# A new order for batch 0 of a Sinkhorn attention and ResMLP kernel: GpSimd products behind the weight loads, K copies and exponentials first, V1 mix inside the first channel layer

## The chip, the cores and the metric

The kernel runs on one core of one Trainium2 chip. The metric is device microseconds (us) of one execution. A profiled execution also shows a span, from the first to the last instruction, which is about 1.8 us shorter than its time. Every execution of the result and of the experiments, and each profile, comes with the mean clock that the TensorE was granted over its span, where 1.0 is full speed.

A run is slow where it is over 1.5% above the fastest of the same kernel in the same call.

## The reference

There are two parts: a sorted block attention and an MLP block that takes its output. Batch is 4, heads 8, sequence 768 in 8 blocks of 96, head size 64, and the MLP width 512.

```python
# attention
P = sort_net                                # 8 x 8 per batch and head
for _ in range(5):                          # exp, then rows and columns normalized
    ...
k_sorted = einsum('bhij,bhjcd->bhicd', P, k_blocks)
v_sorted = einsum('bhij,bhjcd->bhicd', P, v_blocks)
attn = softmax(q_blocks @ k_sorted^T / 8)   # per block of 96
x = attn @ v_sorted                         # -> (batch, 768, 512)
# MLP
a1  = alpha1 * x + beta1
tok = einsum('ts,bsd->btd', w_tok, a1)      # w_tok is 768 x 768
u   = x + lam * tok
a2  = alpha2 * u + beta2
out = u + lam * (relu(a2 @ w_ch1) @ w_ch2)
```

## The kernel before

The tensor engine (PE) works nearly all the time. Batches 1 to 3 run their attention among the channel layers of the batch before, so the PE always has large matmuls at hand. Batch 0 has no batch before it. Its attention consists of small matmuls that wait for one another, and the weight preparation is done in the same stretch: the token weights are copied into a sorted order (`wtp`), turned by the PE (`wtok_ps`) and copied back (`w_tokT`).

In the code, in which some short lines are joined, `pe`, `dve`, `act` and `pool` are TensorE, VectorE, ScalarE and GpSimd. Their instructions stay in program order where `fixed` is set. So the order of the calls below is the order in each engine's queue.

```python
    def prep_affine():                       # two products on GpSimd, 128x512 f32 each
        pool.tensor_tensor(a1lB[:], a1lB[:], lamB[:], ALU.mult)
        pool.tensor_tensor(b1lB[:], b1lB[:], lamB[:], ALU.mult)

    def spin(ps, n):                         # n dummy matmuls, 128x512
        ...

    def load_weights():                      # GpSimd issues these DMAs
        for g in range(4):
            pool.dma_start(W1p[...], ...)
        load_raw(1, 1)
        for g in range(4):
            pool.dma_start(W2p[...], ...)
            if g == 0:
                prep_affine()                # behind the first W2p issue

    def mix_heads(kv, h4, out):              # K or V of batch 0, mixed; two copies out of PSUM
        for lo, hi, copy in ((0, 4, dve.tensor_copy), (4, 6, act.copy)):
            ...

    def sort_wtok(n):                        # two copies SBUF -> SBUF: 128x1152 and 128x384, f16
        for lo, hi, base in ((0, 96, 0), (96, 128, TAIL)):
            dve.tensor_copy(t_[:, :, :, lo:hi], wt16[...])

    def prep_wtok(which, eng):               # six transposes by the PE, one copy PSUM -> SBUF
        for ks in which:
            ...
            eng(w_tokT[:, ks, :], pst[:])

    # ---- order of batch 0 (start cut)
    load_weights()
    mixing_matrices(1)
    turn_v0(0, dve.tensor_copy); mix_k0(0); mix_k0(1); turn_v0(1, dve.tensor_copy)
    sc0(0, 0, 2)                             # scores; the last argument is a number of dummy matmuls
    sc0(0, 1, 2); mix_k0(2); turn_v0(2, dve.tensor_copy)
    sc0(1, 0, 1); pv0(0, 0)                  # pv0: probabilities times V, writes x_ps, then x
    sc0(1, 1, 1); pv0(0, 1); mix_k0(3); turn_v0(3, dve.tensor_copy)
    sc0(2, 0, 1); pv0(1, 0)
    sort_wtok(0)
    sc0(2, 1, 1); pv0(1, 1)
    sort_wtok(1)
    prep_wtok(range(1), dve.tensor_copy)     # the PE waits here for sort_wtok(0)
    sc0(3, 0); pv0(2, 0)
    # ... the rest of w_tokT and x, then the token matmuls tok_ps (128x512)
    mix_v(1, 1, range(0, 4), ...)            # V of batch 1, four of six parts, before the channel layer
    moe_h(0, 0, range(6))                    # first channel layer: h_ps
    mix_v(1, 1, range(4, 6), ...)
    moe_h(0, 0, range(6, HT))
    for kk in range(3):                      # three output blocks (ch_ps) of the first half of batch 0,
        moe_ch(0, 0, (kk,))                  # all before the attention of batch 1
        mix_k(1, gs=(kk,))
        ...
```

The softmax here doesn't subtract the row's maximum and nothing guards it: scores larger than these inputs give would overflow.

Of the kernel before, what the change touches and what calls it, by code (L numbers as in the profile page):

```python
# [16 lines left out]
def kernel(  # L17
# [23 lines left out]
    NB = sort_net.shape[-1]  # L41
# [5 lines left out]
    HT = HID // 128  # L47
# [40 lines left out]
    def psb(shape, dtype, name):  # L88
        return psB.tile(shape, dtype, name=name, tag="psB")
# [63 lines left out]
    def prep_affine():  # L153
        pool.tensor_tensor(a1lB[:], a1lB[:], lamB[:], ALU.mult)
        pool.tensor_tensor(b1lB[:], b1lB[:], lamB[:], ALU.mult)
# [99 lines left out]
    def load_weights():  # L255
        for g in range(4):
            pool.dma_start(W1p[:, :, g * 512:(g + 1) * 512], w1v[:, :, g * 512:(g + 1) * 512])
        load_raw(1, 1)
        for g in range(4):
            pool.dma_start(W2p[:, g * 4:(g + 1) * 4, :], w2v[:, g * 4:(g + 1) * 4, :])  # L260
            if g == 0:
                prep_affine()



# [3 lines left out]
    def mixing_matrices(b):  # L269
        rep = psa([128, NB * NB], FT, "rep_ps")  # L270
        pe.matmul(
            rep[:],
            ebh[:, b, :, :, :].rearrange("p a h j -> p (a h j)"),
            P16[:].rearrange("p i j -> p (i j)"),
            start=True, stop=True,
        )
        sel = att.tile([128, NB, NB], FT, name="sel", tag="sel", bufs=2)
        dve.tensor_tensor(
            sel[:], rep[:].rearrange("p (i j) -> p i j", j=NB),
            mskj[:].unsqueeze(1).to_broadcast([128, NB, NB]), ALU.mult,  # L280
        )
        red = att.tile([128, NB], FT, name="red", tag="red", bufs=2)
        dve.tensor_reduce(red[:], sel[:], AXX, ALU.add)
        big = const([128, 16, NB], F16, f"bigP_{b}")
        dve.tensor_tensor(
            big[:],
            mskb[:].rearrange("p a b -> p (a b)").unsqueeze(2).to_broadcast([128, 16, NB]),
            red[:].unsqueeze(1).to_broadcast([128, 16, NB]),
            ALU.mult,
        )  # L290
        bigP[b] = big
        bgv = const([128, 16, NB], F16, f"bigV_{b}")
        dve.tensor_tensor(
            bgv[:],
            mskv[:].unsqueeze(2).to_broadcast([128, 16, NB]),
            red[:].unsqueeze(1).to_broadcast([128, 16, NB]),
            ALU.mult,
        )
        bigV[b] = bgv
# [74 lines left out]
                    else:  # L374
                        act.copy(dst, src)

    def mix_heads(kv, h4, out):

        raw = raw_of[(0, kv)]
        dst = out.rearrange("p i (t r) -> p t i r", r=16)  # L380
        for lo, hi, copy in ((0, 4, dve.tensor_copy), (4, 6, act.copy)):
            mps = psb([128, hi - lo, 128], FT, "m_ps")
            for t6 in range(lo, hi):
                for h2 in range(2):
                    h = 2 * h4 + h2
                    pe.matmul(
                        mps[h2 * 64:(h2 + 1) * 64, t6 - lo, :], raw[:, h, t6, :],
                        bigH[:, h, :, :].rearrange("p i r -> p (i r)"), start=True, stop=True,
                    )
            copy(dst[:, lo:hi], mps[:].rearrange("p t (i r) -> p t i r", r=16))  # L390

    def mix_k0(h4):
        if 0 not in kT_of:
            kT_of[0] = att.tile([128, H4 * NB, BLK], F16, name="kT", tag="kT", bufs=2)
        mix_heads(0, h4, kT_of[0][:, h4 * NB:(h4 + 1) * NB, :])

    vT0 = []

    def mix_v0(h4):
        vT0.append(moep.tile([128, NB, BLK], F16, name=f"vT_{h4}", tag="u32", bufs=9))  # L400
        mix_heads(1, h4, vT0[h4][:])

    def turn_v0(h4, copy):
        vps = psb([BLK, NB, 2, D], F16, "vt_ps")
        for i in range(NB):
            pe.transpose(vps[:, i, :, :].rearrange("p a d -> p (a d)"), vT0[h4][:, i, :], ident16[:])
        copy(
            Vs[0][:, 2 * h4 * NB:(2 * h4 + 2) * NB, 0:D].rearrange("p (a i) d -> p i a d", a=2), vps[:],
        )
# [46 lines left out]
                    recip[:, lo:hi].unsqueeze(3).to_broadcast([BLK, hi - lo, 2, D]), ALU.mult,  # L456
                )

    def pv_tiles(h4, g, et):

        bank = psb([128, 4, 128], FT, "x_ps")[:].rearrange("p a x -> p (a x)")
        xps = bank[:, 0:6 * GRP].rearrange("p (a i g) -> p a i g", i=3, a=2)
        for rows, cols, i in ((slice(0, BLK), BLK, 0), (slice(BLK, 128), 32, 3)):
            for h2 in range(2):
                for ii in range(3):
                    vi = 3 * g + ii if i == 0 else 6 + g
                    lhsT = et[:, h2, ii, :] if i == 0 else et[:, h2, 3, 32 * ii:32 * ii + 32]
                    pe.matmul(
                        xps[rows, h2, ii, 0:D + 1], lhsT, Vs[0][:, (2 * h4 + h2) * NB + vi, 0:D + 1],
                        start=True, stop=True,  # L470
                    )
        recip = att.tile([128, 2, 3], FT, name="recip", tag="recip0", bufs=3)
        dve.reciprocal(recip[:], xps[:, :, :, D])
        dve.tensor_tensor(
            x_of[0][:, 3 * g:3 * g + 3, h4 * 128:(h4 + 1) * 128].rearrange("p i (a d) -> p a i d", d=D),
            xps[:, :, :, 0:D], recip[:].unsqueeze(3).to_broadcast([128, 2, 3, D]), ALU.mult,
        )
# [26 lines left out]
    def sort_wtok(n):  # L504

        t_ = moep.tile([128, NT, 2, 128], F16, name=f"wtp_{n}", tag="a2T", bufs=3)
        wtp.append(t_)
        for lo, hi, base in ((0, 96, 0), (96, 128, TAIL)):
            w = hi - lo
            dve.tensor_copy(  # L510
                t_[:, :, :, lo:hi],
                wt16[:, :, base + 2 * n * w:base + (2 * n + 2) * w].rearrange("p t (k c) -> p t k c", c=w),
            )
# [10 lines left out]
    def prep_ab2():  # L524
        tps = psb([128, 2 * CT], FT, "ab2_ps")
        pe.transpose(tps[:], ab2[:], ident32[0:2 * CT, 0:2 * CT])
        act.copy(ab2col[:], tps[:])
# [140 lines left out]
    def sc0(h4, g, spins=0):  # L668
        ets[(h4, g)] = emit_scores(0, h4, g, spins)

    def pv0(h4, g):
        pv_tiles(h4, g, ets[(h4, g)])

    x_of[0] = moep.tile([128, NT, C], F16, name="x128", tag="x128", bufs=2)
    mixing_heads()
# [3 lines left out]
    for h4 in range(1, H4):  # L679
        mix_v0(h4)  # L680
    load_weights()
    mixing_matrices(1)
    turn_v0(0, dve.tensor_copy)
    mix_k0(0)
    mix_k0(1)
    turn_v0(1, dve.tensor_copy)
    sc0(0, 0, 2)
    sc0(0, 1, 2)
    mix_k0(2)
    turn_v0(2, dve.tensor_copy)  # L690
    sc0(1, 0, 1)
    pv0(0, 0)
    sc0(1, 1, 1)
    pv0(0, 1)
    mix_k0(3)
    turn_v0(3, dve.tensor_copy)
    sc0(2, 0, 1)
    pv0(1, 0)
    sort_wtok(0)
    sc0(2, 1, 1)  # L700
    pv0(1, 1)
    sort_wtok(1)
    prep_wtok(range(1), dve.tensor_copy)
    sc0(3, 0)
    pv0(2, 0)
    prep_wtok(range(1, 2), dve.tensor_copy)
    sort_wtok(2)
    sc0(3, 1)
    pv0(2, 1)
    prep_wtok(range(2, 4), act.copy)  # L710
    pv0(3, 0)
    prep_wtok(range(4, 5), dve.tensor_copy)
    prep_wtok(range(5, 6), act.copy)
    pv0(3, 1)
    prep_ab2()
    prep_rs()
    moe_start(0)
    moe_row(range(2, NT))
# [4 lines left out]
    for kt in range(2):  # L723
        dve.scalar_tensor_tensor(
            u_of[0][kt][:], b1lB[:], rs[:, kt:kt + 1], x_of[0][:, kt, :], op0=ALU.mult, op1=ALU.add
        )
    moe_tok(0, range(3))
    tok_part(0, 3)
    tok_part(0, 4)
    moe_turn(0, 0)  # L730
    tok_part(0, 5)
    mix_v(1, 1, range(0, 4), (dve.tensor_copy, act.copy))
    pe.fixed = act.fixed = False
    order = [pe.last, act.last]
    moe_tok(0, range(3, NT), done=True)
# [2 lines left out]
    stack = ExitStack()  # L738
    for eng in order:
        stack.enter_context(tc.issue_after(eng.ins))  # L740
    moe_h(0, 0, range(6))
    mix_v(1, 1, range(4, 6), (dve.tensor_copy,))
    pool.tensor_copy(gate[:], Vs[1][0:1, 0, 0:2])
    load_raw(2, 1)
    load_raw(2, 0)
    pool.fixed = False
    moe_h(0, 0, range(6, HT))
    moe_turn(0, 1)
    stack.close()
    pe.fixed = True  # L750
    for kk in range(3):
        moe_ch(0, 0, (kk,))
        mix_k(1, gs=(kk,))
        for h4 in ((0,), (1, 2), (3,))[kk]:
            turn_q(1, h4, dve.tensor_copy)
    pe.fixed = False
    for b in range(1, B):
        if b > 1:
            if b > 2:
                cross_q(b)  # L760
            mixing_matrices(b)
            mix_v(b)
            if b == 2:
                opened = pool.tensor_copy(gate[:], Vs[0][0:1, 0, 0:2])
                with tc.issue_after(opened.ins):
                    load_q(3)
                    load_raw(3, 1)
                    load_raw(3, 0)
            mix_k(b)
        emit_attention(b)  # L770
        if b > 1:
            moe_h(b - 1, 0)
            moe_ch(b - 1, 0)
        moe_h(b - 1, 1)
        moe_a(b)
        moe_ch(b - 1, 1)
        if b == 1:
            load_q(2)
            cross_q(2)
# [33 lines left out]
```

## Time and profile before

| | kernel before |
|---|---|
| time, three runs | 278.16, 278.46, 278.55 us; median 278.46 |
| the profiled run | 282.29 us (span 280.5 us, mean clock 0.975) |
| PE busy | 266.7 us, 95% of the span |
| longest PE wait | 3.67 us, for VectorE's copy wtp, at 27.7 us |
| clock at half speed | from 31.0 to about 44.6 us |
| token matmuls of batch 0 start | 41.90 us |
| token matmuls of batch 1 end | 105.70 us |
| from there to the end | 174.8 us |

These are the head of the page of the kernel before, the PE's line of busy times, and two lines of slices. In the slices each digit stands for a fortieth of the span (7 us); PE is its busy tenths, PEclk its granted clock in tenths.

```profile
span 280.5 us, 5152 instructions
PE 266.7 (95%) x2057; PEld 149.2 (53%) x2057; DVE 160.1 (57%) x332; ACT 126.1 (45%) x233; POOL 92.1 (33%) x100
PE   8889599999999799999999999999999999999993
PEclk9999758999999999999999999999999999999999
```

The PE is 95% busy, so only a little can be gained by filling its gaps. The clock line shows the other loss: in the fifth to seventh slices (28 to 49 us) the PE is granted only 7, 5 and 8 tenths of its speed, and in the sixth and seventh it is called busy all the same.

The timeline of the kernel before around 27 us has the columns start, duration, engine, line, operation, written and read tile, shape, count, and in brackets the idle time before it and what ended it. All operations are recorded in one helper, so the line is always L65 and the tiles tell them apart.

```profile
26.98 0.74 PE L65 MATMUL x_ps<-Vs_96,et 96*96 96x65 f16 x12
...
27.16 4.17 DVE L65 COPY wtp_580<-wt_100 128x1152 f16<-128x1152 f16 x2
...
28.00 1.33 POOL L65 TENSOR_TENSOR a1lB<-a1lB,lamB 128x512 f32<-128x512 f32 x1
29.23 1.31 POOL L65 TENSOR_TENSOR b1lB<-b1lB,lamB 128x512 f32<-128x512 f32 x1
...
31.39 0.82 PE L65 MATMUL wtok_ps<-ident_72,wtp_580 128*128 128x128 f16 x6 [3.67 <-DVE wtp_580 L65]
...
35.02 0.62 DVE L65 COPY wtp_657<-wt_100 128x1152 f16<-128x1152 f16 x2
```

VectorE's two sort copies take 4.17 us. GpSimd's two products (28.00 to 30.54 us) run in that time. The PE has nothing from 27.72 to 31.39 us: it waits for the first sorted tile. The view of that tile gives the shortest, the median and the longest of the two copies, in ns:

```profile
L65 DVE COPY wtp_580<-wt_100 x2: 535/2123/3711, 27.2 to 30.8; 128x1152 f16<-128x1152 f16 x1, 128x384 f16<-128x384 f16 x1
```

The large copy (128x1152) took 3711 ns. The third pair of the same shapes, at 35.02 us where GpSimd does nothing, took 0.62 us for both; there neither copy took more than 0.45 us, against 3.71. This trace shows only that the long copy and the products overlap, not that the products stretch the copy (the collision, below).

The next view is the busy time of the engines in windows of 1 us: window, length, then busy us and number of instructions for PE, PEld, DVE, ACT and POOL, then the granted clock, the DMA share and GB/s.

```profile
30.00:31.00 1.00, 0.00 (x0) 0.00 (x0) 1.00 (x2) 0.00 (x0) 1.00 (x2) 0.97 1.24 207
31.00:32.00 1.00, 0.61 (x6) 0.56 (x6) 0.96 (x4) 0.00 (x0) 1.00 (x3) 0.50 1.23 206
...
44.00:45.00 1.00, 1.00 (x5) 0.35 (x3) 0.48 (x1) 0.75 (x2) 1.00 (x2) 0.70 1.23 205
45.00:46.00 1.00, 1.00 (x7) 0.45 (x5) 0.28 (x2) 0.00 (x0) 1.00 (x2) 1.00 1.27 219
```

The clock falls to 0.50 shortly before the end of the pause (30.9 us, in windows of 0.2 us) and is back at 44.6 us. The matmuls from 31.4 to 41.9 us take longer there: twelve x_ps matmuls 1.06 us instead of 0.67 in the chain.

The waits of the PE (us in total, times, longest) show two more that the change addresses: batch 1's token matmuls wait for x, and the V mix for a copy of itself.

```profile
PE wtok_ps L65 <- DVE wtp_580 L65: 3.7, 1, 3.7
PE tok_ps L65 <- DVE x_1203 L65: 1.4, 2, 0.8
...
PE v_ps L65 <- DVE vA L65: 0.3, 1, 0.3
```

The chain of waits (start, us, what) gives the marks: the start of batch 0's token matmuls and the end of batch 1's.

```profile
41.90 7.88 PE tok_ps L65 x30
...
98.20 7.50 PE tok_ps L65 x34
105.70 10.36 PE ch_ps L65 x48
```

### The profile page before, as it was taken

What the parts mean: (1) busy time and instruction counts of PE and PEld (TensorE: products, weight loads), DVE (VectorE), ACT (ScalarE), POOL (GpSimd) and SP (SyncE); (2) the same over time, 40 slices, a digit from 0 to 9 for tenths busy, and PEclk for the clock granted to TensorE, in tenths of its full rate; (3) what the DMA queues carried; (4) which work ended last, traced back from release to release, by engine and by line L of the source; (5) the groups of instructions that cost most, each with busy time, mean ns of one, the idle gap of its engine ahead of it and who ended that gap; (6) DMA issues with size and microseconds to landing.
All of it is one profiled execution on the core that took longest, in us unless ns stands there. A gap on an engine that the chain in (4) does not pass through costs nothing.

```text
span 280.5 us, 5152 instructions
## 1 busy us (share of the span) xinstructions
PE 266.7 (95%) x2057; PEld 149.2 (53%) x2057; DVE 160.1 (57%) x332; ACT 126.1 (45%) x233; POOL 92.1 (33%) x100
## 2 busy tenths in 40 slices
PE   8889599999999799999999999999999999999993
PEld 2467484555556444455466544554566445545542
DVE  6878947633765898770368386651465874023023
ACT  2456145783358522388056430783076313703700
POOL 8525608800745171502943603400425400000000
PEclk9999758999999999999999999999999999999999
DMA  6999999979999905469999143399210242012012
GB/s 77 184 209 251 212 205 197 182 157 88 154 215 122 106 19 89 115 142 89 137 211 177 37 78 75 90 141 72 76 40 2 47 102 75 2 37 75 2 37 75
DMA packets 62423, 30.88 MB, mean 110 GB/s; under 512 B 48888, under 2 KB 58112, under 8 KB 62400
## 3 DMA queue, kind: packets, MB, share of 16 engines
q0 software_dynamic: 23024, 15.60, 38.6%
q1 hardware_dynamic: 39376, 14.96, 32.5%
q8 instruction: 16, 0.26, 0.4%
q14 instruction: 7, 0.06, 0.1%
HBM read 32.78 MB, written 8.65 MB: 148 GB/s over the span
## 4 chain that ended last, share of the span: by engine, by line
PE 85%; DVE 8%; ACT 4%; issue 1%; DMA 1%; DVEq 0%
PE ch_ps L65 29%; PE h_ps L65 27%; PE tok_ps L65 11%; PE x_ps L65 5%; PE sc_ps L65 4%; ACT kT L65 2%; PE wtok_ps L65 2%; DVE wtp_580 L65 1%; DVE x_1203 L65 1%; PE v_ps L65 1%; PE k_ps L65 1%; PE q_ps L65 1%; PE m_ps L65 1%; ACT et L65 1%; PE vt_ps L65 1%
## 5 line engine op out<-in xcount | busy, mean ns | idle before, releaser
L65 ACT ACTIVATE hTa<-h_ps 128x384 bf16<-128x384 f32 x96 | 46.1, 493 | 52.3 <-PE h_ps L65 51.4
L65 PE MATMUL ch_ps<-W2p,hTa 128*128 128x512 bf16 (+2 forms) x300 | 66.6, 371 | 0.0
L65 PEld LDWEIGHTS <-W1p 128*128 128x128 bf16 x512 | 47.6, 98 | 30.7 <-issue 1.1
L65 DVE TENSOR_TENSOR ch_ps<-ch_ps,lamB 128x512 f32<-128x512 f32 (+2 forms) x25 | 16.9, 675 | 63.8 <-PE ch_ps L65 61.1
L65 PEld LDWEIGHTS <-hTa 128*128 128x128 bf16 x300 | 28.6, 98 | 32.3
L65 ACT ACTIVATE et<-sc_ps 96x768 f16<-96x768 f32 x32 | 25.1, 807 | 23.1 <-PE sc_ps L65 22.7
L65 PEld LDWEIGHTS <-w_tokT 128*128 128x128 f16 x180 | 15.2, 101 | 18.9 <-issue 2.9
L65 PE MATMUL ch_ps<-W2p,hTb 128*128 128x512 bf16 (+2 forms) x100 | 25.0, 370 | 0.0
L65 DVE TENSOR_TENSOR tok_ps<-tok_ps,a1lB 128x512 f32<-128x512 f32 x24 | 16.6, 692 | 9.7 <-PE tok_ps L65 9.6
L65 PEld LDWEIGHTS <-et 96*96 96x96 f16 (+1 forms) x288 | 17.5, 128 | 3.5 <-issue 0.4
L65 DVE CAST kT<-k_ps 64x512 f16<-64x512 f32 x24 | 16.5, 688 | 3.4 <-PE k_ps L65 3.0
L65 ACT ACTIVATE hTb<-h_ps 128x384 bf16<-128x384 f32 x32 | 15.4, 497 | 4.7 <-PE h_ps L65 4.3
L65 PEld LDWEIGHTS <-hTb 128*128 128x128 bf16 x100 | 9.6, 98 | 10.9
L65 DVE RECIPROCAL recip<-x_ps 96x8 f32<-96x8 f32 (+1 forms) x32 | 6.2, 196 | 14.5 <-PE x_ps L65 14.1
L65 PEld LDWEIGHTS <-kT 64*96 64x96 f16 x256 | 8.9, 124 | 9.9 <-issue 4.0
L65 PE MATMUL sc_ps<-qT,kT 64*96 64x96 f16 x256 | 12.6, 217 | 0.4
L65 PE MATMUL h_ps<-a2T_800,W1p 128*128 128x384 bf16 x64 | 12.9, 327 | 0.0
L65 PE MATMUL h_ps<-a2T_2219,W1p 128*128 128x384 bf16 x64 | 12.2, 327 | 0.1
L65 PE MATMUL h_ps<-a2T_2220,W1p 128*128 128x384 bf16 x64 | 12.1, 326 | 0.0
L65 PE MATMUL h_ps<-a2T_1504,W1p 128*128 128x384 bf16 x64 | 11.7, 327 | 0.0
L65 PE MATMUL h_ps<-a2T_1505,W1p 128*128 128x384 bf16 x64 | 11.6, 326 | 0.0
L65 PE MATMUL x_ps<-Vs_96,et 96*96 96x65 f16 (+1 forms) x160 | 11.4, 222 | 0.0
(273 smaller groups left out, 390.9 us busy)
## 6 DMA issues: line engine op xcount, KB each, us to landing
out_dram<-ost SPq DMA_DIRECT2D x23, 192.0 KB, 2.2
vscr<-vA SPq DMA_DIRECT2D x6, 384.0 KB, 4.1
W1p<-in_moe_w_ch_dram POOLq DMA_DIRECT2D x4, 512.0 KB, 9.7
W2p<-in_moe_w_ch_dram POOLq DMA_DIRECT2D x4, 512.0 KB, 15.9
Vs_98<-vscr SPq DMA_DIRECT2D x4, 384.0 KB, 8.2
qn<-in_q_dram POOLq DMA_DIRECT2D x12, 128.0 KB, 4.8
out_dram<-ost SPq DMA_DIRECT2D x23, 64.0 KB, 2.0
wt_100<-in_moe_w_tok_dram POOLq DMA_DIRECT2D x1, 864.0 KB, 15.2
```

The lines of the kernel that those rows point to most:

```text
L65: ins = getattr(self.eng, name)(*args, **kwargs)
```

## The change

Its intent is to take the collision and the pause out of batch 0, and to find the PE work for the attention of batch 1. The products go behind the last weight-load issue; ScalarE takes the larger half of each K copy, so that the first exponential comes earlier, and the fourth V turn; the sort copies move between the products of probabilities and V; V of batch 1 is mixed part by part inside the first channel layer; the third output block is kept for the attention of batch 1. The number of dummy matmuls in this stretch goes from eight to ten.

```diff
         for g in range(4):
             pool.dma_start(W2p[:, g * 4:(g + 1) * 4, :], w2v[:, g * 4:(g + 1) * 4, :])
-            if g == 0:
-                prep_affine()
 # ... mix_heads takes its two copy engines as an argument
-        mix_heads(0, h4, kT_of[0][:, h4 * NB:(h4 + 1) * NB, :])
+        mix_heads(0, h4, kT_of[0][:, h4 * NB:(h4 + 1) * NB, :], (act.copy, dve.tensor_copy))
 # ... pv_tiles takes a number of dummy matmuls (spins)
     load_weights()
-    mixing_matrices(1)
     turn_v0(0, dve.tensor_copy)
     mix_k0(0)
     mix_k0(1)
+    sc0(0, 0, 1)
     turn_v0(1, dve.tensor_copy)
 # ...
+    pv0(1, 0)
     sc0(2, 0, 1)
-    pv0(1, 0)
     sort_wtok(0)
+    pv0(1, 1)
     sc0(2, 1, 1)
-    pv0(1, 1)
     sort_wtok(1)
     prep_wtok(range(1), dve.tensor_copy)
+    pv0(2, 0)
+    sort_wtok(2)
     sc0(3, 0)
-    pv0(2, 0)
     prep_wtok(range(1, 2), dve.tensor_copy)
-    sort_wtok(2)
+    pv0(2, 1)
     sc0(3, 1)
-    pv0(2, 1)
+    prep_affine()
+    turn_v0(3, act.copy)
     prep_wtok(range(2, 4), act.copy)
-    pv0(3, 0)
+    pv0(3, 0, 2)
     prep_wtok(range(4, 5), dve.tensor_copy)
     prep_wtok(range(5, 6), act.copy)
-    pv0(3, 1)
     prep_ab2()
+    pv0(3, 1, 2)
 # ...
     moe_tok(0, range(3))
+    mixing_matrices(1)
 # ...
-    mix_v(1, 1, range(0, 4), (dve.tensor_copy, act.copy))
 # ...
-    moe_h(0, 0, range(6))
-    mix_v(1, 1, range(4, 6), (dve.tensor_copy,))
+    moe_h(0, 0, range(5))
+    for n in range(6):
+        moe_h(0, 0, range(5 + n, 6 + n))
+        mix_v(1, 1, range(n, n + 1), (dve.tensor_copy,))
 # ...
-    for kk in range(3):
+    for kk in range(2):
         moe_ch(0, 0, (kk,))
-        mix_k(1, gs=(kk,))
+        mix_k(1, gs=((0, 1), (2,))[kk])
 # ...
         emit_attention(b)
-        if b > 1:
+        if b == 1:
+            moe_ch(0, 0, (2,))
+        else:
             moe_h(b - 1, 0)
             moe_ch(b - 1, 0)
```

More of the change, by code (lines that the diff above doesn't have):

```diff
@@ L375, in mix_k, with mix_heads @@
                         act.copy(dst, src)
-    def mix_heads(kv, h4, out):
+    def mix_heads(kv, h4, out, copies):
         raw = raw_of[(0, kv)]
         dst = out.rearrange("p i (t r) -> p t i r", r=16)
-        for lo, hi, copy in ((0, 4, dve.tensor_copy), (4, 6, act.copy)):
+        for (lo, hi), copy in zip(((0, 4), (4, 6)), copies):
             mps = psb([128, hi - lo, 128], FT, "m_ps")
@@ L400, in mix_v0 @@
         vT0.append(moep.tile([128, NB, BLK], F16, name=f"vT_{h4}", tag="u32", bufs=9))
-        mix_heads(1, h4, vT0[h4][:])
+        mix_heads(1, h4, vT0[h4][:], (dve.tensor_copy, act.copy))
     def turn_v0(h4, copy):
@@ L457, in emit_pv, with pv_tiles @@
                 )
-    def pv_tiles(h4, g, et):
+    def pv_tiles(h4, g, et, spins=0):
         bank = psb([128, 4, 128], FT, "x_ps")[:].rearrange("p a x -> p (a x)")
+        spin(bank, spins)
         xps = bank[:, 0:6 * GRP].rearrange("p (a i g) -> p a i g", i=3, a=2)
@@ L669, in sc0, with pv0 @@
         ets[(h4, g)] = emit_scores(0, h4, g, spins)
-    def pv0(h4, g):
-        pv_tiles(h4, g, ets[(h4, g)])
+    def pv0(h4, g, spins=0):
+        pv_tiles(h4, g, ets[(h4, g)], spins)
     x_of[0] = moep.tile([128, NT, C], F16, name="x128", tag="x128", bufs=2)
@@ L685 @@
     mix_k0(1)
+    sc0(0, 0, 1)
     turn_v0(1, dve.tensor_copy)
-    sc0(0, 0, 2)
-    sc0(0, 1, 2)
+    sc0(0, 1, 1)
     mix_k0(2)
+    pv0(0, 0)
+    sc0(1, 0, 1)
     turn_v0(2, dve.tensor_copy)
-    sc0(1, 0, 1)
-    pv0(0, 0)
+    pv0(0, 1)
     sc0(1, 1, 1)
-    pv0(0, 1)
     mix_k0(3)
-    turn_v0(3, dve.tensor_copy)
+    pv0(1, 0)
     sc0(2, 0, 1)
-    pv0(1, 0)
     sort_wtok(0)
+    pv0(1, 1)
     sc0(2, 1, 1)
-    pv0(1, 1)
     sort_wtok(1)
     prep_wtok(range(1), dve.tensor_copy)
+    pv0(2, 0)
+    sort_wtok(2)
     sc0(3, 0)
-    pv0(2, 0)
     prep_wtok(range(1, 2), dve.tensor_copy)
-    sort_wtok(2)
+    pv0(2, 1)
     sc0(3, 1)
-    pv0(2, 1)
+    prep_affine()
+    turn_v0(3, act.copy)
     prep_wtok(range(2, 4), act.copy)
-    pv0(3, 0)
+    pv0(3, 0, 2)
     prep_wtok(range(4, 5), dve.tensor_copy)
     prep_wtok(range(5, 6), act.copy)
-    pv0(3, 1)
     prep_ab2()
+    pv0(3, 1, 2)
     prep_rs()
@@ L746 @@
     pool.fixed = False
-    moe_h(0, 0, range(6, HT))
+    moe_h(0, 0, range(11, HT))
     moe_turn(0, 1)
@@ L750 @@
     pe.fixed = True
-    for kk in range(3):
+    for kk in range(2):
         moe_ch(0, 0, (kk,))
-        mix_k(1, gs=(kk,))
-        for h4 in ((0,), (1, 2), (3,))[kk]:
+        mix_k(1, gs=((0, 1), (2,))[kk])
+        for h4 in range(2 * kk, 2 * kk + 2):
             turn_q(1, h4, dve.tensor_copy)
```

## The prediction

> **What bounds the kernel now.** TensorE: busy 266.7 of 280.5 us, 85% of the chain of waits. In batch 0 three things cost it time.
>
> 1. The timeline shows VectorE's first copy of sorted token weights (128x1152, tile wtp) starting at 27.16 us and lasting 3.71 us; the third pair of such copies takes 0.62 us for both. Meanwhile GpSimd runs its two parameter products (28.00 to 30.54 us); the copy ends 0.3 us after them. [...] The PE waits 3.67 us for the copy (waits view).
> 2. After that the granted clock (1 us windows) is 0.50 from 31 to 44.4 us. [...] The small matmuls of 31.4 to 41.9 do not bring it back; the 512-wide token matmuls do, after 2.5 us. Twelve x_ps matmuls take 1.06 us there, 0.67 us before the pause.
> 3. Attention of batch 1 runs out of filler: TensorE idles 0.68 + 0.76 us at 96 to 98.2 us for VectorE's x. Mixing V1 costs another 0.35 us at 52.5.
>
> **What the change does.** The GpSimd products go behind the last weight-load issue: at about 30.3 us, not 28.0. The K copy's larger half goes to ScalarE (about 0.59 us), so the first exponential starts near 18.4 us instead of 19.86. The sort copies start near 25 us (the token weights have landed at about 24.7) and, by my count of VectorE's work, end near 29.3, before the products. The fourth V turn moves to ScalarE (about 0.9 us). Dummy matmuls: 10 instead of 8, at about 0.22 us. V1 mixing moves into the first channel layer: same work, no wait. The third output block of batch 0 (16 matmuls, 3.45 us) becomes filler of batch 1's attention: in the new order 25 rather than 11 channel matmuls lie between the last x_ps and the token matmuls (4 us, against a need of about 2.2).
>
> **Sum (estimates from the durations above).** Replaying batch 0 at full clock in the new order, the token matmuls start near 35 us instead of 41.9: -6.9. Thirty of them take 6.5 us rather than 7.88: -1.4. V1 wait: -0.3. Attention filler: -1.4. Together -10.0; all lies on TensorE's chain, and behind it TensorE is nearly full to the end, so the end moves too. I hold back 0.7 us for new waits at 30 to 34 us (bank reuse, ScalarE's copies). Predicted **269.2 us**, 80% range **267.0 to 272.2**. Faster by over 2%: 0.90; within 2%: 0.09; slower: 0.01.
>
> **What would show it.** Right: the first wtp copy pair takes 0.6 to 0.9 us; no TensorE gap above 1.5 us between 17 and 36; granted clock 1.0 in the windows 30 to 45; first token matmul at 34 to 37; GpSimd's products at about 30 to 33 with no sort copy stretched; no 1.4 us gap before batch 1's token matmuls; from there to the end as long as before within 1 us.
>
> **What would make it wrong.** (a) The clock falls anyway: 26 to 34 us is small matmuls with short waits, and four dummies may not be enough; that gives back up to 5 us (about 273 to 275). (b) A VectorE copy, say of w_tokT, meets the products and stretches by up to 2.6 us. (c) TensorE arrives 7 us earlier at the first layers: W2p lands at 43 to 50 us, K1/Q1 near 57, needed near 60; V1 through DRAM near 68, needed near 72. Slack is thin, and a wait there costs directly.

That the products stretch the copy, and that the pause halves the clock, were assumptions. The sum rests on them, and e2, e4 and e11 test them.

## The result and the profile after

| | before | after |
|---|---|---|
| median of four runs each | 278.5 us (278.16 to 279.6) | 271.24 us (271.13 to 271.27) |
| ratio of fast runs, 95% | | 0.9732 (0.9705 to 0.9759): faster |
| profiled run | 282.29 us, span 280.5, clock 0.975 | 271.13 us, span 269.4, clock 1.0 |
| token matmuls of batch 0 start | 41.90 us | 34.62 us |
| token matmuls of batch 1 end | 105.70 us | 94.27 us |
| from there to the end | 174.8 us | 175.1 us |

A ratio here and below is the mean time of one kernel's fast runs over the mean of the other's fast runs of the same rounds, so it is not quite the ratio of the medians quoted.

The head of the page after, its PE line and the same two lines of slices:

```profile
span 269.4 us, 5147 instructions
PE 260.8 (97%) x2049; PEld 145.5 (54%) x2059; DVE 155.0 (58%) x333; ACT 126.0 (47%) x232; POOL 92.4 (34%) x100
PE   7899999999999999999999999999999999999993
PEclk9999999999999999999999999999999999999999
```

The PE's slices at 5 tenths (the fifth) and 7 tenths (the fourteenth) are gone, and so are the slow slices of the clock. (The 7 at the head is the 1.4 us before the first matmul, in slices that are now shorter.) The PE is busy for 97% of a shorter span.

The timeline of the kernel after, in the columns explained above:

```profile
24.86 0.94 DVE L65 COPY wtp_556<-wt_100 128x1152 f16<-128x1152 f16 x2
...
26.40 0.62 DVE L65 COPY wtp_587<-wt_100 128x1152 f16<-128x1152 f16 x2
...
28.09 0.89 DVE L65 COPY wtp_614<-wt_100 128x1152 f16<-128x1152 f16 x2
...
30.48 0.59 PE L65 MATMUL x_ps<-ident_72 128*128 128x512 f16 x2 [0.48 <-ACT Vs_96 L65]
...
31.79 0.74 POOL L65 DMA_DIRECT2D W2p<-in_moe_w_ch_dram  x1 [1.81 <-DMA W1p<-in_moe_w_ch_dram]
...
32.54 1.28 POOL L65 TENSOR_TENSOR a1lB<-a1lB,lamB 128x512 f32<-128x512 f32 x1
...
33.78 1.27 POOL L65 TENSOR_TENSOR b1lB<-b1lB,lamB 128x512 f32<-128x512 f32 x1
```

The sort copies come at 24.86, 26.40 and 28.09 us, and no pair takes more than 0.94 us. GpSimd's products run at 32.54 to 35.05 us, behind them all. They are two microseconds later than predicted, because GpSimd waited 1.81 us for W1p to land before it could issue the last W2p load. The longest wait of the PE that is left in this stretch is 0.48 us, for ScalarE's copy of V.

Windows of 5 us of the kernel after, columns as above:

```profile
30.00:35.00 5.00, 4.52 (x80) 3.53 (x80) 2.11 (x6) 2.85 (x6) 3.20 (x3) 1.00 1.25 213
35.00:40.00 5.00, 5.00 (x25) 2.17 (x24) 4.75 (x8) 3.30 (x6) 4.17 (x5) 1.00 1.09 206
40.00:45.00 5.00, 5.00 (x37) 2.88 (x35) 4.09 (x11) 3.17 (x6) 5.00 (x6) 1.00 1.24 205
```

The clock is 1.00 throughout, where the kernel before had 0.50. The longest waits of the PE after are these; the waits for wtp, x and vA are no longer in the list:

```profile
PE spin_ps L65 <- POOL ident_72 L65: 1.4, 1, 1.4
PE x_ps L65 <- ACT Vs_96 L65: 0.5, 1, 0.5
```

In the chain of waits the first thirty token matmuls take 3.91 + 2.70 = 6.61 us, against 7.88 before, and those of batch 1 are one piece of 36 without a break:

```profile
34.62 3.91 PE tok_ps L65 x18
38.66 2.70 PE tok_ps L65 x12
...
86.50 7.77 PE tok_ps L65 x36
```

From profile to profile the gain is 280.5 - 269.4 = 11.1 us. From median to median it is 7.2. The experiments had to say which of the two is the gain of the change, and which parts of the change it comes from.

### The profile page after: what moved, and what is told of

Read it like the earlier page. It is cut to its first block, busy times and chain, and to the rows that moved or that the text cites. A ratio compares the mean times of both kernels' runs of the same rounds, so it can differ in the third digit from the quotient of the medians.

```text
span 269.4 us, 5147 instructions
## 1 busy us (share of the span) xinstructions
PE 260.8 (97%) x2049; PEld 145.5 (54%) x2059; DVE 155.0 (58%) x333; ACT 126.0 (47%) x232; POOL 92.4 (34%) x100
## 4 chain that ended last, share of the span: by engine, by line
PE 89%; ACT 4%; DVE 4%; issue 1%; DMA 1%; DVEq 0%; ACTq 0%
PE ch_ps L65 30%; PE h_ps L65 30%; PE tok_ps L65 12%; PE x_ps L65 6%; PE sc_ps L65 4%; ACT kT L65 2%; PE v_ps L65 2%; PE k_ps L65 1%; PE q_ps L65 1%; ACT et L65 1%; DVE csum L65 1%; DVE P_78 L65 1%; PE m_ps L65 1%; DVE rsum L65 1%; PE wtok_ps L65 1%
## 5 line engine op out<-in xcount | busy, mean ns | idle before, releaser
L65 PEld LDWEIGHTS <-et 96*96 96x96 f16 (+1 forms) x288 | 16.2, 120 | 3.4 <-issue 0.3
L65 POOL DMA_DIRECT2D qn<-in_q_dram x12 | 10.8, 921 | 4.1 <-PE q_ps L65 3.4
```

Source lines behind the costliest of these rows:

```text
L65: ins = getattr(self.eng, name)(*args, **kwargs)
```

## The experiments

Theory: the products stretch a sort copy and make a pause for the PE; the pause halves the clock, and both are charged to the PE. Added to that are about 1.7 us in batch 1's attention and in the mix of V.

Rivals: (1) the clock and not the pause, or the pause and not the clock, does the damage; (2) the products are harmless and the new order alone brings the gain; (3) the extra dummy matmuls keep the clock up; (4) the difference of 3.8 us between the profiled run and the median is chance.

The kernels without a fall of the clock spread over 0.1 to 0.6 us. So their medians are compared with the 271.24 us of the kernel after; this is less strict than a comparison in the same rounds, and the ratio with the kernel before stands beside it. The kernel after was in none of the experiments' calls, and these were on three chips (e1 to e8 on one, e9 to e11 on another, e12 on a third), so differences of a few tenths of a us from 271.24 are not shown to be real by the times alone.

### e1: the kernel before once more

No edit.

> The kernel before, unchanged. The profiled run on which the prediction rested took 282.29 us, while the three other runs had a median of 278.46. Theory A: the length of the half-clock stretch after the pause differs from run to run[...], so the granted clock of the 278 us runs is above the 0.975 of the profiled one, by about 3.8 us x 0.5 lost clock / 280 = near 0.985 to 0.99, and time falls as mean clock rises. Rival B: the profiled run was slower for another reason (its clock the same, 0.975, in all runs). New profile: same DVE copy of 3.7 us, half-clock stretch of some 8 to 13 us.

Measured: median 279.87 us over six runs (275.87 to 283.61), three of them fast and three slow; ratio of the fast runs 0.9942 (0.9874 to 1.0011). Its profile, of a fast run, has a span of 277.4 us at a clock of 0.981. In it the collision hit another copy. This is its timeline:

```profile
27.16 0.62 DVE L65 COPY wtp<-wt 128x1152 f16<-128x1152 f16 x2
...
28.46 3.52 DVE L65 COPY wtp<-wt 128x1152 f16<-128x1152 f16 x2
...
28.66 1.28 POOL L65 TENSOR_TENSOR a1lB<-a1lB,lamB 128x512 f32<-128x512 f32 x1
...
32.49 1.52 PE L65 MATMUL wtok_ps<-ident,wtp 128*128 128x128 f16 x12 [1.75 <-DVE w_tokT L65]
```

The first pair of sort copies takes 0.62 us here, and the second pair 3.52 us. In this execution GpSimd had waited 0.81 us for the landing of b1lB before, and its products began at 28.66 us, not at 28.00. The pause of the PE is 1.75 us instead of 3.67, and the half clock is shorter: from 31.6 to 41.9 us. Two windows of 4 us inside it (columns as above):

```profile
32.00:36.00 4.00, 3.51 (x36) 3.29 (x37) 3.78 (x11) 1.52 (x2) 1.40 (x2) 0.50 1.23 219
36.00:40.00 4.00, 4.00 (x57) 2.71 (x56) 2.24 (x5) 2.38 (x6) 0.45 (x1) 0.50 1.07 200
```

So the same program pays a different amount in each execution. All 50 runs of the kernel before in the experiments (274.93 to 283.71 us, median 279.96) fall on a ladder of the granted clock:

| mean clock of the run | runs | mean time, us |
|---|---|---|
| 0.998, 0.999 | 4 | 275.72 |
| 0.993 | 7 | 277.22 |
| 0.987 | 5 | 278.93 |
| 0.981, 0.982 | 17 | 280.2 |
| 0.975 | 3 | 282.24 |
| 0.966, 0.970 | 6 | 283.4 |

(Eight runs lie between these rungs.) One rung is about 0.006 of the clock. The time at half clock, read from windows of 0.2 us, is 13.65 us in the profile before, 10.25 us in e1's and 3.4 us in e3's below: four, three and one times the shortest of them. By an estimate from these figures a stretch of 3.4 us, as part of 280 us, is 3.4 x 0.5 / 280 = 0.006 of the mean clock. So rival (4) is right in so far as chance decides the rung, but the rung decides the time. The profile before stood on the rung 0.975 at 282.29 us. The clocks of the three runs behind the median of 278.46 us are not recorded; by the ladder their time belongs between 0.987 and 0.993.

### e2: the products alone, moved behind the loads

Kernel before with this edit:

```diff
         for g in range(4):
             pool.dma_start(W2p[...], ...)
-            if g == 0:
-                prep_affine()
+        prep_affine()
```

> The kernel before with one move only: GpSimd's two parameter products behind the last W2p issue. Theory[...]: the first wtp copy pair falls to below 1 us, no 3.67 us pause, clock 1.0 throughout, gain 6 us or more of the 7.2 measured (272.5 or lower), unless the products then meet a later sort copy. Rival (the order of K copies, exponentials and V turns brings the gain): gain below 2 us, 276.5 or higher.

Measured: median 274.82 us (274.32 to 278.19; the run at 278.19 had a clock of 0.993); ratio 0.9869 (0.9816 to 0.9922). The first pair of sort copies takes 0.82 us, the PE waits 0.32 us for it, and the token matmuls start at 35.33 us. By the medians, moving two instructions of GpSimd brings 5.1 us of the 8.7 between the typical run before (279.96) and the kernel after. By the fast runs alone it brings 1.3%, about half of the 2.7% of the whole change. Rival (2) falls: the order is not the only source of the gain.

The timeline of e2 shows the short pair, and answers a fear of the prediction as well, its point (b):

```profile
27.08 0.82 DVE L65 COPY wtp<-wt 128x1152 f16<-128x1152 f16 x2
...
32.41 1.28 POOL L65 TENSOR_TENSOR a1lB<-a1lB,lamB 128x512 f32<-128x512 f32 x1
...
32.93 0.55 DVE L65 COPY w_tokT<-wtok_ps 128x768 f16<-128x768 f16 x1
```

A copy of w_tokT runs in the middle of the first product and takes 0.55 us, as VectorE's three in the profile before do (0.54 to 0.56 us). It reads PSUM. So this copy out of PSUM was a safe neighbour of the products, where the copies from SBUF to SBUF were not (3.49 to 4.17 us for a pair that met them, in the profile before, e1, e3 and e4). What makes the difference is not shown.

### e3: the products back, everything else as after

Kernel after with this edit:

```diff
             pool.dma_start(W2p[...], ...)
+            if g == 0:
+                prep_affine()
 # ...
     sc0(3, 1)
-    prep_affine()
     turn_v0(3, act.copy)
```

> The kernel after with the products put back between the first and second W2p issue. Theory[...]: they run at about 28.2 to 30.7 us and now meet the THIRD sort copy (28.1 us), which stretches to end near 31; the normalizing of x behind it holds a PSUM bank, so TensorE idles 1.5 to 2.5 us near 30 us. If that is too short to halve the clock: 273 to 274 us; if the clock falls: 275 to 278. Rival (the products do not matter, order does): within 0.5 us of 271.2.

Measured: median 274.01 us (272.72 to 274.41, clocks 0.992 to 0.997); ratio 0.9813 (0.9773 to 0.9852). That is 2.8 us slower than the kernel after. The timeline of e3:

```profile
27.99 3.49 DVE L65 COPY wtp<-wt 128x1152 f16<-128x1152 f16 x2
...
28.16 1.30 POOL L65 TENSOR_TENSOR a1lB<-a1lB,lamB 128x512 f32<-128x512 f32 x1
...
31.99 0.49 PE L65 MATMUL wtok_ps<-ident,wtp 128*128 128x128 f16 x6 [2.46 <-DVE w_tokT L65]
```

With the earlier copies of the new order the products meet the third pair (3.49 us). The PE then waits 2.46 us for a w_tokT copy that stands behind it. The clock is halved for 3.4 us only, from 32.95 to 36.35 us. So the new order lessens the damage, 2.8 us instead of 5.1, and does not remove it. What the moving of the products is worth depends on the order around them: 5.1 of 8.7 us taken first (e2), 2.8 taken last.

### e4: the pause kept, the clock held up

Kernel before with seventeen dummy matmuls where the PE waits:

```diff
     sort_wtok(1)
+    spin(psb([128, 512], FT, "spin_ps")[:], 17)
     prep_wtok(range(1), dve.tensor_copy)
```

> The kernel before with 17 dummy matmuls of 512 columns (17 x 0.216 = 3.7 us) put on TensorE into the pause, the products unmoved. The VectorE copy still takes 3.7 us and the weight transposes still start near 31.4 us, but the clock stays at 1.0. Theory (most of the loss is the clock that the pause takes away, not the pause): gain 4 to 6 us in the profile against the profile of the kernel before, 273 to 275 us as a time. Rival (the pause itself is the loss): no gain, 278 or above.

Measured: median 277.31 us (277.22 to 278.98); ratio 0.9955 (0.9911 to 0.9999). As a time this missed what was expected. The profile shows that the edit did its work, in two lines of the timeline:

```profile
27.06 3.94 DVE L65 COPY wtp<-wt 128x1152 f16<-128x1152 f16 x2
...
27.55 3.84 PE L65 MATMUL spin_ps<-ident 128*128 128x512 f16 x17
```

The dummies fill the pause, the copy is nearly as long as before (3.94 us for the pair, 4.17 before), the clock is 1.0 in the whole run, and the span is 275.4 us, 5.1 less than the profile before (4 to 6 was expected of the clock). The time missed because the 4 to 6 us were again taken from a median of runs of higher clocks. Five of the six runs lie within 0.21 us of each other; without the half clock the spread of the kernel before is gone. So clock and pause are both charged, and can be told apart: against the profile before, 5.1 us are the clock, and from e4 to e2 (275.4 to 273.1) 2.3 us are the pause. Rival (1) falls in both forms. Against the typical run before, the same subtraction gives 279.96 - 277.31 = 2.65 us. That is no clean size of the clock alone, because the pause differs between executions too (3.67 us in the profile before, 1.75 in e1's), while e4 has the long copy of the profile before: the four best runs of the kernel before, at clocks of 0.998 and 0.999, took 274.93 to 276.16 us, less than e4. That they had a short pause as well is likely but was not seen, as they have no profile.

### e5 and e6: without the dummy matmuls

Kernel after; e5 takes all ten dummies out, e6 the last four:

```diff
 # e5 and e6
-    pv0(3, 0, 2)
+    pv0(3, 0)
-    pv0(3, 1, 2)
+    pv0(3, 1)
 # e5 alone: also the six in the scores, in the manner of
-    sc0(0, 0, 1)
+    sc0(0, 0)
```

> The kernel after without its ten dummy matmuls among batch 0's scores and products with V. Theory A (the small matmuls between 17 and 34 us hold the clock by themselves, as they did in the run with the products moved alone, which had none after 27 us): clock stays 1.0, up to 10 x 0.22 = 2.2 us less, 269 to 270.5, less where a dummy filled a wait. Rival B (the dummies hold the clock): a half-clock stretch appears between 20 and 37 us, time 273 or more and a wide spread over the runs.

> The kernel after without the four dummy matmuls before the last two products with V (about 30.5 and 32.5 us). A: they only cost time (4 x 0.22 = 0.9 us): 270.3 to 270.9. B: without them the clock falls near 33 us in some or all runs: 272 or more, spread over 1 us.

Measured: e5 271.04 us (270.29 to 272.32), ratio 0.965 (0.9603 to 0.9696); e6 270.82 us (270.7 to 272.31), ratio 0.9648 (0.9602 to 0.9693). In e5 the clock fell in two of six runs (0.984 and 0.987), and in e6 two of six runs are 1.0 and 1.5 us above the median. So rival (3) falls as the cause of the gain: most runs keep their clock without the dummies. But the dummies seem to have a use as insurance, since the kernel after has a spread of 0.14 us over four runs and these have 2.0 and 1.6 over six each. That e5 is not clearly faster although it does less is shown by its profile: the PE comes to the first sorted tile earlier and waits 1.17 us for it there. The landing of the token weights was not read in e5; by GpSimd's waits for it in seven other profiles it comes at 24.2 to 24.7 us.

### e7: without the filler of batch 1's attention

Kernel after, the third output block back where it was (and the turns of Q with it):

```diff
-    for kk in range(2):
+    for kk in range(3):
         moe_ch(0, 0, (kk,))
-        mix_k(1, gs=((0, 1), (2,))[kk])
+        mix_k(1, gs=(kk,))
 # ...
-        if b == 1:
-            moe_ch(0, 0, (2,))
-        else:
+        if b > 1:
```

> The kernel after with batch 0's third output block (and the split of K1 mixing and Q turns) back ahead of batch 1's attention. Theory: TensorE waits for VectorE's x twice before batch 1's token matmuls, 1.4 us together as before; time 272.4 to 273.0, batch 0 unchanged. Rival (the wait was hidden or is made up later): within 0.4 us of 271.2.

Measured: 272.93 us (272.82 to 273.42), ratio 0.9712 (0.9669 to 0.9755): 1.7 us above the kernel after, as expected. In its profile the token matmuls of batch 0 start at 34.62 us as after, and those of batch 1 end at 96.24 us instead of 94.27. A wait for x in batch 1 is back, one of 0.77 us, where the kernel before had two of 1.4 us together. The other 1.2 us of the 1.97 are charged as busy time of the PE and are not located.

### e8: V of batch 1 mixed where it was

Kernel after, with the V mix and its matrices back:

```diff
     load_weights()
+    mixing_matrices(1)
     turn_v0(0, dve.tensor_copy)
 # ...
-    mixing_matrices(1)
 # ...
+    mix_v(1, 1, range(0, 4), (dve.tensor_copy, act.copy))
 # ...
-    moe_h(0, 0, range(5))
-    for n in range(6):
-        moe_h(0, 0, range(5 + n, 6 + n))
-        mix_v(1, 1, range(n, n + 1), (dve.tensor_copy,))
+    moe_h(0, 0, range(6))
+    mix_v(1, 1, range(4, 6), (dve.tensor_copy,))
```

> The kernel after with V1's matrices and mixing back at their old places (matrices among batch 0's K and V work, four mixing matmuls between the token matmuls and the first channel layer). The four mixing matmuls took 1.54 us before the first layer, 0.86 at full rate: expected +0.5 to +1.0 us, 271.7 to 272.2, the first exponential of batch 0 about 0.2 us later. Rival (no effect): within 0.3 us.

Measured: 271.87 us (271.79 to 272.04), ratio 0.9673 (0.9626 to 0.9719): 0.6 us above the kernel after, as expected. But the place was not the expected one. Of it 0.48 us lie in batch 0, where the token matmuls start at 35.10 us instead of 34.62, and only 0.2 in the mix. The small VectorE operations that build the matrices stood before the first exponential in the queue, which came at 18.89 us instead of 18.41. Taking them out of there is most of what this part brings.

### e9: the K copies as before

Kernel after with the halves of the K copies exchanged again:

```diff
-        mix_heads(0, h4, kT_of[0][...], (act.copy, dve.tensor_copy))
+        mix_heads(0, h4, kT_of[0][...], (dve.tensor_copy, act.copy))
```

> The kernel after with the larger half of each K copy of batch 0 back on VectorE and the smaller on ScalarE. Theory: the first exponential starts about 0.3 to 0.6 us later, but the sort copies cannot start before the token weights have landed (near 24.8 us), so the token matmuls start within 0.3 us of 34.5 and the time stays within 0.4 us of 271.2. Rival (copies and exponentials first is a main part of the gain): 272.2 or more.

Measured: 271.17 us (271.16 to 271.26), ratio 0.9769 (0.973 to 0.9808): the same as the kernel after. The first exponential, which was expected later, starts at 18.46 us against 18.41. This part of the change shows no worth by itself.

### e10: the products and the last copies nearer

Kernel after with the products behind the third W2p issue, a w_tokT turn moved up, and one dummy less:

```diff
             pool.dma_start(W2p[...], ...)
+            if g == 2:
+                prep_affine()
 # ...
-    prep_affine()
     turn_v0(3, act.copy)
     prep_wtok(range(2, 4), act.copy)
-    pv0(3, 0, 2)
     prep_wtok(range(4, 5), dve.tensor_copy)
+    pv0(3, 0, 1)
```

> An attempt at a better version: the kernel after with the products one W2p issue earlier (they would run at about 30.0 to 32.5 us, behind the last sort copy at 29.0, ahead of an issue[...]), the fifth weight transpose ahead of the seventh product with V (it fills TensorE's 0.48 us wait for ScalarE's V copy), and one dummy fewer. Expected gain 0.5 to 0.9 us over the kernel after (270.3 to 270.7), clock 1.0. Failure would be: the products meet the third sort copy in some runs (273 to 274), or no change because the token stage is bound by VectorE.

Measured: 270.88 us (270.85 to 271.13), ratio 0.976 (0.972 to 0.9799). It is 0.36 us below the kernel after, less than expected. It was run at another time. The issue that the products were to go ahead of had waited 1.81 us for W1p in the kernel after. Here the third W2p issue itself waited 1.39 us for W1p, so the products ran at 31.08 to 33.57 us, and the PE still waited 0.61 us for ScalarE's copy of V.

### e11: the sort copies on another engine

Kernel before, with the first two pairs of sort copies on ScalarE and the products where they were:

```diff
-    sort_wtok(0)
+    sort_wtok(0, act.copy)
 # ...
-    sort_wtok(1)
+    sort_wtok(1, act.copy)
```

> The kernel before with the first two pairs of sort copies on ScalarE, the products at their old place. Theory[...]: ScalarE's two copies take their plain time, about 1.1 and 0.5 us by ScalarE's 0.80 us for 768 columns, although GpSimd's products run at the same time (28.0 to 30.5); TensorE's pause is below 2 us. Rival (the products slow any SBUF copy, or the source itself arrives late): a ScalarE copy of 3 us or more. Time: 274 to 279 us, with ScalarE's exponentials now later.

Measured: 274.29 us over four runs (274.17 to 275.99), ratio 0.9901 (0.9834 to 0.9968), span 272.4 us. This tells whether the products stretch any such copy or only one on VectorE. The timeline of e11:

```profile
26.48 1.55 ACT L65 COPY wtp<-wt 128x1152 f16<-128x1152 f16 x2
...
28.46 1.29 POOL L65 TENSOR_TENSOR a1lB<-a1lB,lamB 128x512 f32<-128x512 f32 x1
...
28.64 1.56 ACT L65 COPY wtp<-wt 128x1152 f16<-128x1152 f16 x2
```

The second pair on ScalarE runs beside the products and takes 1.56 us. The first pair, with no product beside it, took 1.55. So the products did not stretch the copies on ScalarE, where on VectorE a pair that met them took 3.49 to 4.17 us. It also shows that the collision can be taken away with the products left in place.

### e12: e10 and two further moves

The edit of e10, with the fourth V turn ahead of the last scores and one more w_tokT copy on VectorE:

```diff
+    turn_v0(3, act.copy)
     sc0(3, 1)
-    turn_v0(3, act.copy)
-    prep_wtok(range(2, 4), act.copy)
-    prep_wtok(range(4, 5), dve.tensor_copy)
+    prep_wtok(range(2, 3), act.copy)
+    prep_wtok(range(3, 5), dve.tensor_copy)
     pv0(3, 0, 1)
```

> The tighter version again, with the fourth V turn one step earlier (before the last scores, so ScalarE's 1.0 us copy of it ends near 29.9 rather than 30.4) and the fourth weight transpose copied by VectorE, idle there, instead of ScalarE. In the tighter version TensorE still waited 0.61 us for ScalarE's V copy. Expected: that wait below 0.2 us, token matmuls near 33.6 us instead of 34.2, time 270.2 to 270.6 if the token stage follows; no change from 270.9 if it is bound by VectorE's row and sum work behind b1lB (ready at 33.6).

Measured: 270.72 us (270.66 to 271.0), ratio 0.9728 (0.967 to 0.9786). It was run at another time. It just missed what was expected and has the lowest median, 0.5 us (0.2%) below the kernel after, with no overlap of their ranges; but by their profiles the token matmuls of batch 0 start at 34.49 us against 34.62, a gain of 0.13 us. The ratio of e10 and e12 to the kernel before does not show this, because the kernel before stood on different rungs. The PE still waits 0.35 us for ScalarE's copy of V and 0.2 us for a sort copy.

## Why the prediction was right or wrong

The prediction was 269.2 us with a range of 267.0 to 272.2, and faster by over 2% with a chance of 0.90. Measured were 271.24 us and a ratio of 0.9732. So the middle is 2.0 us too low.

The chain view allows a full account from profile to profile. Each term is a difference of two profiles of the table below.

| profile | token matmuls of batch 0 start | batch 1's end | rest | span |
|---|---|---|---|---|
| before | 41.90 | 105.70 | 174.8 | 280.5 |
| e1 (before again) | 38.45 | 102.61 | 174.8 | 277.4 |
| e4 (clock held, pause kept) | 38.23 | 100.64 | 174.8 | 275.4 |
| e2 (products moved alone) | 35.33 | 97.75 | 175.4 | 273.1 |
| e3 (after, products back) | 37.88 | 97.53 | 175.1 | 272.6 |
| after | 34.62 | 94.27 | 175.1 | 269.4 |

- Half clock on the small matmuls of batch 0, before to e4: 41.90 - 38.23 = 3.67 us (by chance the same figure as the pause).
- The pause of the PE, e4 to e2: 38.23 - 35.33 = 2.90 us. (The spans differ by only 2.3, since the rest of e2 is 0.6 us longer.)
- The rest of the new order in batch 0, e2 to after: 35.33 - 34.62 = 0.71 us, of which e8 puts 0.48 on the matrices for V1.
- Half clock on the token matmuls: the middle stretch (first mark to second) is 63.80 us before and 62.41 in e4, a difference of 1.39 us.
- Filler for batch 1 and V1 mix: the middle stretch goes on from 62.42 us in e2 to 59.65 after, 2.77 us. By the middle stretches of e7 (96.24 - 34.62 = 61.62) and e8 (94.94 - 35.10 = 59.84), 1.97 us of it are the filler and 0.19 the mix; 0.6 us no run isolates.
- The rest, 174.8 to 175.1 us (175.4 in e2): 0.3 us given back. No experiment tells why, and this stays open.

The sum is 3.67 + 2.90 + 0.71 + 1.39 + 2.77 - 0.3 = 11.1 us, the difference of the spans.

Point by point:

1. "TensorE waits 3.67 us for the copy" because of the products, and "the granted clock is 0.50" after it: both right. e2 and e3 show the products as the cause, e11 shows that the same copies on ScalarE are not stretched (1.56 us beside the products, 1.55 without), and e4 tells the clock's part from the pause's.
2. "The token matmuls start near 35 us": 34.62. "Thirty of them take 6.5 us rather than 7.88": 6.61, and 1.39 us saved in the middle stretch. Both right.
3. "V1 wait: -0.3. Attention filler: -1.4": together 1.7 predicted and 2.77 measured, under-sized by about 1 us.
4. "I hold back 0.7 us for new waits at 30 to 34 us": the wait there was 0.48 us, but the start of 34.62 already contains it. Nothing had to be held back.
5. The step that failed is the subtraction: "Together -10.0" was read from a profiled run of 282.29 us and taken from the median of 278.46 us. In those runs, by the ladder of e1, a part of the loss by the clock was not there to be saved. Paired as it should be, profile with profile, the saving was 11.1 us and the estimate, 10.0 less the 0.7 held back, was 1.8 us too small. The baseline was 3.8 us too favourable. The difference of the two errors is the 2.0 us. That they have opposite signs, and so left the range true, is luck. The 1.8 us are mainly the filler and V1 mix (1.07, point 3), the 0.7 held back (point 4) and the earlier start (0.38: 41.90 - 34.62 = 7.28 instead of 6.9), less the 0.3 given back at the end. So the term that was mis-sized is the loss by pause and half clock in the runs of the median. In the profiled run the half clock alone took 5.1 us (e4). By time, going to e4 saves 2.65 us of the typical run of 279.96 us and would save 278.46 - 277.31 = 1.15 of the quoted median.
6. "The first exponential starts near 18.4 us": 18.41, but worth nothing alone. With the K copies exchanged back (e9) it is 18.46 and the time the same, and the sort copies cannot start before the token weights land, at 24.68 us in the profile before and 24.23 in the one after by GpSimd's wait for them.
7. "GpSimd's products at about 30 to 33": at 32.54 to 35.05 us. The prediction did not count the wait of GpSimd's last issue for W1p (1.81 us). It cost no time on the PE's chain.
8. Of the dangers named, (a) a fall of the clock anyway did not appear in the four runs of the kernel after, though e5 shows it in two of six runs without dummies (0.984 and 0.987); (b) did not come true where it could be seen: in e2 a copy of w_tokT out of PSUM met a product and took 0.55 us, as without one (0.54 to 0.56); (c) a late weight did not show among the PE's waits.

## What to carry to other kernels

Before a saving read from a profile is subtracted from a median, check that the profiled run is as long as that median; where it is not, find out what differs between the executions, for it may be the very thing that the change removes. A pair of small GpSimd instructions can cost more than its own length where a large SBUF-to-SBUF copy of VectorE meets it and TensorE waits behind the copy (here 2.5 us of products cost 5.1 us by the medians, e2); put such instructions behind the last of these copies, or the copies on ScalarE (here 1.56 us for a pair beside the products, e11). After a pause of TensorE look at the granted clock in narrow windows, and try large dummy matmuls in the pause (here seventeen of 128x512, with a clock of 1.0, e4), for the clock can cost more than the pause (here 5.1 us against 2.3).

## What the traces show of the clock and of the copies

- The fall of the clock. In the profile before it fell 3.2 us after the last matmul (27.72 to 30.9 us). In e1 the pause was 1.75 us in all, and the clock fell at 31.6 us, after only 0.9 us without any matmul. In e3 the pause was 2.46 us, and the clock fell at 32.95 us, 1.0 us after the matmuls had begun again. So the length of the pause alone does not tell when the clock falls.
- Its return. In the profile before, the PE was called fully busy with small matmuls from 32 to 41.9 us, and the clock stayed at 0.50; it came back at 44.6 us, after 2.7 us of 512-wide token matmuls. In e4 the same small matmuls, from 31.2 to 38.1 us, kept a clock of 1.0: what kept the clock in one run did not bring it back in another. In e3 it came back at 36.35 us, before the token matmuls began (37.88 us), so the return did not need them. What decides it is not shown.
- The half-speed stretches of 13.65, 10.25 and 3.4 us are four, three and one times 3.4 us, to within 0.05 us. Their length changes from run to run: one unchanged kernel took from 274.93 to 283.71 us, 3%.
- The large copy took 3.71 us beside the products, and its end came about 0.3 us after theirs; ScalarE was untouched (1.55 and 1.56 us). Before, the copy is recorded from 27.16 us and the first product from 28.00, and yet the copy, of which the like took at most 0.45 us in the third pair, ended after both products. In the runs with a long copy (before, e1, e3 and e4) GpSimd was issuing loads when the copy began. That is not enough alone: in e2 a pair of sort copies began during the issue of W2p loads (27.03 to 28.58 us), with no product behind it, and took 0.82 us. How the products come to hold up a copy that began before them stays open.
